# Attention with a gated convolution behind it: keys, queries and values loaded by groups of four heads

## The chip, the cores and the metric

The kernel runs on one core of a Trainium2 chip. The metric is the device time of one execution in microseconds (us); the time before is the median of three runs. The profile is that of one execution, and its span goes from the first to the last instruction.

## What is computed

`q`, `k` and `v` are float32 of 8 batches x 12 heads x 448 rows x 64. Attention has one more term in the denominator; its output, heads side by side, goes through a projection to three parts of 768, a convolution over the sequence by Fourier transform, two gates and a last projection:

```python
scores = scale * np.matmul(q, k.transpose(0, 1, 3, 2))
m = np.max(scores, axis=-1, keepdims=True)
e = np.exp(scores - m)
attn = e / (np.sum(e, axis=-1, keepdims=True) + np.exp(-m) + 1e-09)
x = np.matmul(attn, v)                        # then heads side by side: (8, 448, 768)
proj = x @ w_proj                             # three parts x1, x2, x3
x2_conv = np.fft.irfft(np.fft.rfft(x2, n=S, axis=1) * np.fft.rfft(filter_fft, n=S, axis=0), n=S, axis=1)
return (x1 * x2_conv * x3) @ w_out
```

## The kernel before, in words

The work is cut into tasks: a load, a set of matmuls, a copy out of PSUM. Each names its engine, what it needs and what it makes. A planner (`Plan`, the table `plan.ORDER`) fixes the order of the tasks on each engine when the program is built; `plan.FLIP` names the copies that go to the other of VectorE (DVE) and ScalarE (ACT). On the chip every engine then runs its own list in that order, and waits where an operand is not ready. Where the planner expects a hole in TensorE's early work, it puts filler matmuls on a tile of zeros (L1566, after 38 at the very start, L1574).

**Attention** goes by pairs of heads, 48 in all; i is the pair's number. Keys lie with the 64 features of two heads on the 128 partitions. For each pair there are three blocks of 128 keys (L947, four 64x64 matmuls to a set), and the last 64 keys of two neighbouring pairs share a fourth block (L952). Each set is followed by one exponential of 128x896 on ScalarE (L966), which writes an `e` buffer (seven of them) or, for the shared block, `er`. The outputs are 65 columns wide, since a column of ones beside the values gives the denominator: L977 for the shared rows, L997 for the three blocks. A tiny write (`sink` on ScalarE, `sinks` on GpSimd, L987) orders the two halves of a bank. VectorE divides (L1010 to L1012) into `xb`, and DMA transposes (L1056; TensorE in batch 0) make `xT`.

**The dense part** of a batch has the projections (L1175 for the convolved part, L1273 for the two gates), the transforms by tables `ft`, `fr`, `bt` (L1157, L1223, L1319), VectorE's products and sums between them, and the output projection L1091, whose result is copied to `osb` and stored by SP's queue (L1406, three buffers in turn).

**Loads of keys, queries and values** are what the change is about. Batches 0 and 1 are "staged" (`staged`): GpSimd's queue casts to bfloat16 on the way, four heads to a DMA (L544 queries in runs of 1024 B, L549 keys and values in runs of 768 B); the first two pairs come as float32 through SP's and ScalarE's queues and are cast by VectorE or GpSimd (L585, L591). TensorE turns keys and queries pair by pair (L621 to L642) and VectorE or ScalarE copies the turned blocks to `kT` and `qT` (L488, L486). Batches 2 to 7 are "loaded" (`loaded`): SP's queue brings each pair's keys and queries as float32 (L747, L727), GpSimd casts them (L759, L733), and DMA transposes on SP's queue turn them (L705 keys, L694 queries); GpSimd's queue brings the values (L754), and GpSimd copies them beside their ones (L771). The last 64 rows of keys and values come apart, in `rests`, in four DMAs of 256 B runs for the keys and four for the values of a batch (L509), and GpSimd casts them (L514, L719). The weights come by GpSimd's queue (L924, L929), the filter too (L836 to L840). The pads between the halves of the `e` buffers are zeroed by GpSimd (L1583, L1584).

## Time and profile before

| what | value |
| --- | --- |
| median of three runs | 372.58 us |
| lowest and highest run | 371.19 and 373.03 us |
| profiled execution, first to last instruction | 370.8 us |
| busy: TensorE, VectorE, ScalarE, GpSimd | 356.4, 274.8, 237.5, 127.6 us |
| DMA packets, bytes | 133958, 61.93 MB |

The execution that was profiled has no time of its own beside its span of 370.8 us; the runs' median lies 1.8 us above it. Rows of the profile name a line of the kernel, the engine, the operation, and the tiles written and read. "<-" at the end of a row names what ended the engine's idle time before it. PEld is TensorE's weight load, which overlaps its matmuls.

### The profile page before, as it was taken

The page shows a single profiled execution, that of the slowest core. Times are in us where ns is not written, and L with a number is a line of the kernel's source. Part 1 is how long each engine was busy: PE and PEld are TensorE (multiplying, and loading weights), DVE is VectorE, ACT ScalarE, POOL GpSimd, SP SyncE. Part 2 cuts the span into 40 slices and gives each one's busy share as a digit, 9 for nine tenths or more (in the row PEclk, how much of TensorE's full clock was granted, in tenths as well). Part 3 has the DMA queues.
Part 4 walks back from the last instruction along what each step waited for, and adds up shares of the span by engine and source line. Part 5 has one row for each costly group of instructions (what it writes and reads, how often), then busy time and mean ns, then how long its engine had stood idle before and what let it go on. Part 6 is the DMA issues. An engine that isn't in the chain of part 4 may idle for free. (4 is left out here: it accounts for less than half of the span.)

```text
span 370.8 us, 10707 instructions
## 1 busy us (share of the span) xinstructions
PE 356.4 (96%) x4300; PEld 211.8 (57%) x4300; DVE 274.8 (74%) x674; ACT 237.5 (64%) x379; POOL 127.6 (34%) x278
## 2 busy tenths in 40 slices
PE   7989999999999979999999999999999999999995
PEld 7666675554555545565555646665565655555552
DVE  5468659982789726897579977689459898779970
ACT  4999876756767548567565657867776561334343
POOL 9984251444625274265537523313100100000000
PEclk9999999999999999999999999999999999999999
DMA  9999999988999999999998799995830074125035
GB/s 169 194 191 204 207 207 205 206 169 160 168 242 156 229 214 208 235 242 192 206 182 202 166 245 192 262 208 122 171 72 1 7 196 89 42 45 170 4 129 172
DMA packets 133958, 61.93 MB, mean 167 GB/s; under 512 B 105165, under 2 KB 130704, under 8 KB 133904
## 3 DMA queue, kind: packets, MB, share of 16 engines
q1 hardware_dynamic: 111552, 48.71, 61.6%
q0 software_dynamic: 22112, 12.26, 25.4%
q8 instruction: 34, 0.56, 0.6%
q10 hardware_dynamic: 240, 0.23, 0.2%
q14 instruction: 20, 0.16, 0.2%
HBM read 43.86 MB, written 11.01 MB: 148 GB/s over the span
## 5 line engine op out<-in xcount | busy, mean ns | idle before, releaser
L966 ACT ACTIVATE e<-psum 128x896 bf16<-128x896 f32 x144 | 126.6, 920 | 40.8 <-PE psum L947 37.3
L1273 PE MATMUL psum<-xT,wproj_bf 128*128 128x448 bf16 x576 | 121.7, 353 | 0.1
L1273 PEld LDWEIGHTS <-wproj_bf 128*128 128x128 bf16 x576 | 53.4, 98 | 47.7 <-issue 5.0
L1091 PE MATMUL psum<-wout_bf,yT 128*128 128x384 bf16 x288 | 54.7, 326 | 0.8 <-DVE g L1288 0.4
L1175 PE MATMUL psum<-xf,wproj_bf 128*128 128x452 bf16 x252 | 53.9, 357 | 0.0
L947 PE MATMUL psum<-qT,kT 64*64 64x448 bf16 x576 | 45.4, 359 | 2.5 <-DVE g L1288 0.7
L997 PEld LDWEIGHTS <-e 128*128 128x128 bf16 x1152 | 42.0, 98 | 9.6 <-issue 5.2
L997 PE MATMUL psum<-vn,e 128*128 128x65 bf16 x1152 | 46.8, 194 | 0.0
L733 POOL CAST nat<-nat 112x512 bf16<-112x512 f32 x36 | 25.4, 708 | 44.7 <-DMA nat<-in_q_dram 41.8
L1241 DVE TENSOR_TENSOR t<-xs,hrs 113x768 bf16<-113x768 bf16 (+1 forms) x64 | 36.4, 578 | 2.9 <-ACT xs L486 2.3
L1288 DVE TENSOR_TENSOR g<-x,psum 128x448 bf16<-128x448 bf16 x48 | 29.2, 616 | 12.1 <-PE psum L1273 10.9
L1091 PEld LDWEIGHTS <-yT 128*128 128x128 bf16 x288 | 26.6, 98 | 19.9 <-issue 1.8
L1175 PEld LDWEIGHTS <-wproj_bf 128*128 128x128 bf16 x252 | 23.2, 96 | 22.2 <-issue 1.1
L486 ACT CAST x<-psum 128x448 bf16<-128x448 f32 (+1 forms) x39 | 20.4, 529 | 22.6 <-PE psum L1273 14.5
L759 POOL CAST nat<-nat 128x384 bf16<-128x384 f32 x36 | 21.5, 598 | 32.2 <-DMA nat<-in_k_dram 31.9
L486 ACT COPY osb<-psum 128x384 f32<-128x384 f32 x39 | 18.2, 486 | 20.1 <-PE psum L1091 15.9
L486 ACT CAST xs<-psum 113x384 bf16<-113x384 f32 (+1 forms) x41 | 19.2, 482 | 15.1 <-PE psum L1223 14.1
L1012 DVE TENSOR_TENSOR xb<-psum,den 128x896 bf16<-128x896 f32 x24 | 26.2, 1091 | 0.8
L486 ACT CAST cr<-psum 128x452 bf16<-128x452 f32 x35 | 18.0, 539 | 11.5 <-PE psum L1319 11.0
L947 PEld LDWEIGHTS <-kT 64*64 64x64 bf16 x576 | 15.6, 105 | 17.1 <-issue 12.9
L966 ACT ACTIVATE er<-psum 128x896 bf16<-128x896 f32 x24 | 22.2, 926 | 4.3 <-PE psum L952 3.5
L987 POOL MEMSET sinks<- 1x1 bf16 x18 | 1.6, 91 | 65.6 <-PE psum L977 65.6
(143 smaller groups left out, 501.3 us busy)
## 6 DMA issues: line engine op xcount, KB each, us to landing
nat<-in_q_dram SPq DMA_DIRECT2D x37, 224.0 KB, 3.8
out_dram<-osb SPq DMA_DIRECT2D x21, 384.0 KB, 3.5
nat<-in_k_dram SPq DMA_DIRECT2D x38, 192.0 KB, 3.9
nat<-in_v_dram POOLq DMA_DIRECT2D x15, 192.0 KB, 6.3
wproj_bf<-in_moe_w_proj_dram POOLq DMA_DIRECT2D x2, 1152.0 KB, 18.1
out_dram<-osb SPq DMA_DIRECT2D x12, 192.0 KB, 2.7
ks<-in_v_dram POOLq DMA_DIRECT2D x9, 192.0 KB, 4.9
rests<-in_k_dram SPq DMA_DIRECT2D x32, 48.0 KB, 4.3
```

The source lines that it names most:

```text
L486: nc.scalar.copy(to, of)
L733: lambda hp=hp, qsrc=qsrc: nc.gpsimd.tensor_copy(qn[:, hp].rearrange("p j (u d) -> p u j d", u=2), qsrc.rearrange("p (u j d) -> p u j d", ...
L759: lambda hp=hp, sv=sv: nc.gpsimd.tensor_copy(kn[:, hp // 2, 3 * (hp % 2) + 1 : 3 * (hp % 2) + 4].rearrange("p j (u d) -> p u j d", u=2), sv),
L947: nc.tensor.matmul(sc[r, u, 0:S], kT[b % 2][c, hp // 2, 3 * turned + t, r], qT[b % 2][c, hp, :])
L966: nc.scalar.activation(to, of, AF.Exp, scale=SCALE)
L997: nc.tensor.matmul(out_bank(u)[:, n + 3 * turned, :], P["e"][1 + t][:, o : o + 128], vn[b % 2][:, hp, 4 * u + t, :], start=False, stop=tur ...
L1012: nc.vector.tensor_tensor(W["xb", b][:, hp // 2].rearrange("p s (u d) -> p u s d", u=2), op[:, :, :, 0:DH], rec[:].unsqueeze(3).to_broadca ...
L1091: nc.tensor.matmul(ops[:n, :DCH], y[:, dt, 0:n], wout_bf[:, dt, ch * DCH : (ch + 1) * DCH], start=(dt == 0), stop=(dt == NDT - 1),)
L1175: nc.tensor.matmul(pps, wproj_bf[:, kt, D + dt * 128 : D + (dt + 1) * 128], W["xf", b][:, :, kt, 0:FQ], start=(kt == 0), stop=(kt == NDT - 1),
L1241: nc.vector.tensor_tensor(t[:K], L["xs", par, ch][:K], h, op=ALU.mult)
L1273: nc.tensor.matmul(p[:, :S], wproj_bf[:, kt, 2 * part * D + dt * 128 : 2 * part * D + (dt + 1) * 128], xT()[:, kt, 0:S], start=(kt == 0), ...
L1288: nc.vector.tensor_tensor(g[:, dt, :], L["x1", dt], p[:, :S], op=ALU.mult)
```

## The change

Four heads form a group: heads 2m, 2m+1, 2m+6 and 2m+7. A pair is now a head and the one six places on. A partition holds seven neighbouring rows of one head, so keys and queries of a group come in runs of 7 x 64 x 4 = 1792 B, two for each of 128 partitions, and the fourth of the seven rows is the shared key block. `rests` and its 64 DMAs are gone.

- Batches 0 and 1: one DMA on GpSimd's queue for a group's keys and one for its queries, 14 turns of 128x64 on TensorE for each, and one copy of 128x896 to `kqT`. Group 0 of batch 0 comes as four float32 loads of 64 partitions, three on SP's and one on ScalarE's queue, and is turned as float32 by 14 matmuls each with a float32 unit matrix (`eye`).
- Batches 2 to 7: one float32 load on SP for keys and one for queries of a group, one cast of 128x896 each on GpSimd, and one DMA transpose of 14 blocks for both, where before keys and queries had their own.
- Values of all batches come by GpSimd's queue in DMAs of 64 partitions with runs of 1024 B (four to a batch, eight in batch 0), cast on the way; one copy to a pair instead of two, and four small copies for the shared rows (eight in batch 0).
- The projection's weights come in two DMAs of 64 partitions each, since the heads stand in another order. The scores read their queries as seven runs of 64 columns. Every exponential puts the rows back in order as it writes. Before the branch SP has 113 instructions instead of 227 and GpSimd 219 instead of 277; TensorE has 23 fillers fewer, 140 bfloat16 turns instead of 160, and 56 float32 ones.
- `plan.ORDER` and `plan.FLIP` are new. The copies that make `fr` can now go to VectorE, and do; the `sink` writes of batch 0 go to GpSimd.

```diff
-    def rows(x, b, hp, n=2):
-        return bass.AP(x.tensor, x[b, 2 * hp].offset, [[3 * DH, 128], [S * DH, n], [1, 3 * DH]])
...
+    def group(x, b, m, par=None):
+        return bass.AP(x.tensor, x[b, 2 * m + (par or 0)].offset, [[PER * DH, 128 if par is None else 64], [NHP * S * DH, 2], [1, PER * DH]])
...
+    def v_load(b, h, n):
+        for r in range(2):
+            nc.gpsimd.dma_start(
+                vroom[64 * r : 64 * r + 64, DH * (4 * h + 1 - r) :][:, 0 : 4 * DH * n].rearrange("p (h x) -> p h x", h=n),
+                bass.AP(v.tensor, v[b, h].offset + 3 * DH * r, [[PER * DH, 64], [S * DH, n], [1, 4 * DH]]),
+            )
...
+    def kq_turn(src, hy):
+        tb = bank2(hy)
+        of = src.rearrange("p (u j d) -> p u j d", u=2, j=PER)
+        for j in range(PER):
+            for u in range(2):
+                nc.tensor.transpose(tb[64 * u : 64 * u + 64, j * 128 : (j + 1) * 128], of[:, u, j], ident_bf)
+
+    def kq_first(x, p, hy):
+        tb, c = bank(hy), slice(64 * p, 64 * p + 64)
+        of = first_kq[x][c].rearrange("p (u j d) -> p u j d", u=2, j=PER)
+        for j in range(PER):
+            for u in range(2):
+                nc.tensor.matmul(tb[64 * u : 64 * u + 64, j * 64 : (j + 1) * 64], of[:, u, j], eye[c, c])
...
+            for x, of in enumerate((k, q)):
+                at = 6 * (b - NSTAGED) + 2 * m + x
+                src = rooms[(2 + at) % 3]
...
+                add("SP", 0.5, 0.0, lambda of=of, src=src, m=m: nc.sync.dma_start(split(src), group(of, b, m)), need=free, make=[("s", b, m, x)],
+                    dma=1.18, run=60)
...
+            add("SP", 2.0, 0.0,
+                lambda m=m: nc.sync.dma_start(
+                    kqT[b % 2][:, m].rearrange("p x j n -> p (x j) n"), kqn[:, m].rearrange("p x j c -> p (x j c)"), transpose=True
+                ),
...
-        nc.gpsimd.dma_start(
-            wproj_bf[:, :, cs], moe_w_proj[:, cs].rearrange("(t p) c -> p t c", p=128)
-        )
+        for c in range(2):
+            nc.gpsimd.dma_start(
+                wproj_bf[64 * c : 64 * c + 64, :, cs], moe_w_proj[c * DCH : (c + 1) * DCH, cs].rearrange("(t p) c -> p t c", p=DH)
+            )
...
-                        nc.tensor.matmul(sc[r, u, 0:S], kT[b % 2][c, hp // 2, 3 * turned + t, r], qT[b % 2][c, hp, :])
+                        nc.tensor.matmul(sc[r, u, 0:S], kq[c, m, 0, 4 * d + t - 1, n], kq[c, m, 1, :, n])
```

**ScalarE, batch 0.** These are rows of ScalarE's list at its start; `e` and `er` are exponentials, `fr` a table, `sink` the tiny write, `kT` turned keys. Before:

```order
L486 COPY kT_89<-psum 128x384
L966 ACTIVATE e_97<-psum 128x2x448
L966 ACTIVATE e_96<-psum 128x2x448
L854 CAST fr<-psum 113x452
L855 ACTIVATE fr<-psum 113x226
L966 ACTIVATE e_98<-psum 128x2x448
L966 ACTIVATE e_99<-psum 128x2x448
L966 ACTIVATE e_100<-psum 128x2x448
L966 ACTIVATE er_103<-psum 128x896
L966 ACTIVATE e_101<-psum 128x2x448
L486 COPY kT_89<-psum 128x384
L966 ACTIVATE e_102<-psum 128x2x448
```

The same place after the change:

```order
L468 CAST kqT_89<-psum 128x7x64 x2
L789 ACTIVATE e_93<-psum 128x2x448
L789 ACTIVATE e_94<-psum 128x2x448
L789 ACTIVATE e_95<-psum 128x2x448
L789 ACTIVATE er_100<-psum 128x896
L789 ACTIVATE e_96<-psum 128x2x448
L789 ACTIVATE e_97<-psum 128x2x448
L789 ACTIVATE e_98<-psum 128x2x448
L789 ACTIVATE e_99<-psum 128x2x448
L789 ACTIVATE e_93<-psum 128x2x448
L468 COPY kqT_89<-psum 128x896
L789 ACTIVATE er_100<-psum 128x896
```

The fr copies and the second key copy have left the run of exponentials, and a copy of a whole group stands behind the ninth.

**GpSimd, the start.** Rows of GpSimd's list after the identity matrix; `vroom` holds values as they land, `vn` values beside their ones, `e` here is the zeroing of the pads. Before, the pads stand ahead of the first load:

```order
L1584 MEMSET e_102 128x64
L544 DMA nat<-in_q_dram 112x4x256
L549 DMA nat<-in_k_dram 128x4x192
L549 DMA nat<-in_v_dram 128x4x192
L591 CAST ldm<-nat 112x2x4x64
L585 CAST ldm<-nat 128x2x3x64
```

After the change ten loads and the first values stand ahead of them:

```order
L488 DMA vroom<-in_v_dram 64x3x256 x2
L537 DMA nat<-in_k_dram 128x2x448
L537 DMA nat<-in_q_dram 128x2x448
L1412 MEMSET vn_92 128x42
L537 DMA nat<-in_k_dram 128x2x448
L537 DMA nat<-in_q_dram 128x2x448
L537 DMA nat<-in_k_dram 128x2x448
L497 COPY vn_91<-vroom 128x2x3x64
L508 COPY vn_91<-vroom 64x2x64
```

The pads have moved from the front of the list to a place behind ten loads and the first copies of values.

**SP, around the first output stores.** Rows of SP's queue; `out_dram` is a store, `rests` the shared rows, `kT`, `qT` and `kqT` turns by DMA, `x` a turn of the dense part. Before, around the second store:

```order
L727 DMA nat<-in_q_dram 112x2x256
L747 DMA nat<-in_k_dram 128x2x192
L1406 DMA out_dram<-osb 128x768
L509 DMA rests<-in_v_dram 64x3x64 x4
L727 DMA nat<-in_q_dram 112x2x256 x2
L747 DMA nat<-in_k_dram 128x2x192
L705 DMA_TRANSPOSE kT_89<-nat 128x11x128
```

After the change, around the first three stores:

```order
L1011 DMA_TRANSPOSE x_2024<-ldm 128x12x128
L1229 DMA out_dram<-osb 128x768
L577 DMA nat<-in_k_dram 128x2x448
L1229 DMA out_dram<-osb 128x768
L587 DMA_TRANSPOSE kqT_90<-nat 128x14x128
L577 DMA nat<-in_k_dram 128x2x448
L1229 DMA out_dram<-osb 128x768
```

The four small loads are gone, and what stands before a store is one load of twice the size, or a turn of 14 blocks.

## The prediction

> **What bounds the kernel now.** The page comes first: who is busy, and is it even over the span?

> ```profile
> PE 356.4 (96%) x4300; PEld 211.8 (57%) x4300; DVE 274.8 (74%) x674; ACT 237.5 (64%) x379; POOL 127.6 (34%) x278
> PE   7989999999999979999999999999999999999995
> DMA  9999999988999999999998799995830074125035
> ```

> TensorE is busy for 96%, with thin slices only at the start and the end; the DMA engines are nearly full for two thirds of the span. The table by stretches sharpens this; its columns after the width are PE, weight loads, DVE, ACT and POOL.

> ```profile
> 0.00:10.00 10.00, 7.87 (x95) 6.78 (x95) 5.96 (x24) 5.29 (x8) 9.29 (x31) 1.00 1.00 170
> 10.00:30.00 20.00, 17.73 (x418) 12.62 (x419) 12.24 (x29) 18.96 (x29) 18.10 (x38) 1.00 1.38 193
> 30.00:100.00 70.00, 69.09 (x902) 41.89 (x899) 50.27 (x124) 51.48 (x85) 28.91 (x59) 1.00 1.11 194
> 100.00:200.00 100.00, 95.83 (x1166) 54.30 (x1164) 75.22 (x181) 66.16 (x100) 45.74 (x100) 1.00 1.13 210
> 200.00:300.00 100.00, 99.73 (x1252) 58.76 (x1254) 78.92 (x185) 68.04 (x106) 25.52 (x53) 1.00 0.71 143
> 300.00:361.00 61.00, 61.00 (x451) 34.59 (x451) 52.15 (x136) 24.04 (x47) 0.09 (x1) 1.00 0.34 95
> ```

> From 30 us on TensorE idles 0.91 us to 100, 4.17 us from there to 200, and 0.27 from there to 361. From 10 to 30 us ScalarE is the full engine (18.96 of 20) and TensorE's time is partly filler. So the change, which leaves the dense matmuls alone, can win in two places only: in ScalarE's run of exponentials before 30 us, and in TensorE's few waits after that. The waits view, TensorE from 30 to 361 us, names these:

> ```profile
> PE psum L977 <- DVE osb L488: 2.5, 2, 2.3
> PE psum L1223 <- DMA x<-ldm: 0.8, 1, 0.8
> PE psum L947 <- DVE g L1288: 0.7, 2, 0.5
> ```

> **The start.** ScalarE's timeline shows batch 0 (21 exponentials of 128x896):

> ```profile
> 8.74 1.73 ACT L966 ACTIVATE e<-psum 128x896 bf16<-128x896 f32 x2 [0.68 <-PE psum L947]
> 10.36 0.54 ACT L854 CAST fr<-psum 113x452 bf16<-113x452 f32 x1
> 10.93 0.36 ACT L855 ACTIVATE fr<-psum 113x226 bf16<-113x226 f32 x1
> 11.19 2.53 ACT L966 ACTIVATE e<-psum 128x896 bf16<-128x896 f32 x3
> 13.79 0.92 ACT L966 ACTIVATE er<-psum 128x896 bf16<-128x896 f32 x1
> 15.40 0.49 ACT L486 COPY kT<-psum 128x384 bf16<-128x384 bf16 x1
> 15.76 0.95 ACT L966 ACTIVATE e<-psum 128x896 bf16<-128x896 f32 x1
> 16.57 0.18 ACT L987 COPY sink<-one 1x1 bf16<-1x1 bf16 x1
> 21.68 0.18 ACT L987 COPY sink<-one 1x1 bf16<-1x1 bf16 x1
> 24.95 2.60 ACT L966 ACTIVATE e<-psum 128x896 bf16<-128x896 f32 x3
> 27.43 0.18 ACT L987 COPY sink<-one 1x1 bf16<-1x1 bf16 x1
> ```

> Three in 2.53 us, 0.92 each, start 0.81 us apart. The first starts at 8.74, the eighth at 15.76, and the last ends at 24.95 + 2.60 = 27.55. In this stretch the change takes from ScalarE the two fr copies (0.54 + 0.36), a key copy (0.49) and three sink copies (3 x 0.18): 1.93 us. It adds one copy of 128x896 from PSUM, which I price as an exponential of that size, 0.92. **Net -1.0 us.** The fr copies and four of the group copies go to VectorE, which has 7.8 us free between 10 and 30; if that cover were gone, the 0.9 would come back.

> Can the exponentials begin as early? The first group's keys and queries now come as four loads of 64 partitions, and TensorE turns them as float32, 14 matmuls a load, where before VectorE or GpSimd cast and TensorE turned in bfloat16. The last of the four old loads had landed when GpSimd cast it:

> ```profile
> 7.23 0.51 POOL L585 CAST ldm<-nat 128x384 bf16<-128x384 f32 x1
> 8.12 0.57 PE L947 MATMUL psum<-qT,kT 64*64 64x448 bf16 x8 [0.34 <-ACT kT L486]
> ```

> The four now move 917 KB instead of 850, so I keep 7.2 us. No row has a float32 matmul; the nearest are these:

> ```profile
> L642 PE MATMUL psum<-ident_bf,nat 112*64 112x112 bf16 x80 | 3.7, 212 | 0.0
> L997 PE MATMUL psum<-vn,e 128*128 128x65 bf16 x1152 | 46.8, 194 | 0.0
> ```

> Packed, they take 3.7/80 = 46 ns each, so 14 take 0.65 us at least; one by one at 212 ns they take 3.0. I take twice the lower end, 1.3, since the operand has twice the bytes and these too go to two halves of the array. The scores of the first head pair stand behind all four turns: 7.2 + 1.3 = 8.5, and 0.62 later (8.12 to 8.74) the first exponential, 9.1 instead of 8.74. The eighth could then start at 9.1 + 7 x 0.81 = 14.8.

> [...]

> The eighth waits for something else as well. GpSimd zeroed the pads of the e buffers from 1.71 to 4.07 us (the first and the last of 14 rows below); now it issues ten loads first, and the eighth score stands in TensorE's queue behind the outputs of the first pair, which need the pads.

> ```profile
> L549 POOL DMA_DIRECT2D nat<-in_v_dram x6 | 4.8, 809 | 0.0
> L544 POOL DMA_DIRECT2D nat<-in_q_dram x5 | 3.7, 743 | 0.0
> L598 POOL COPY vn<-nat 128x192 bf16<-128x192 bf16 x24 | 8.1, 375 | 9.1 <-DMA nat<-in_v_dram 9.0
> ```

> ```profile
> 1.71 0.27 POOL L1583 MEMSET e<- 128x128 bf16 x1
> 3.92 0.15 POOL L1584 MEMSET e<- 128x64 bf16 x1
> ```

> Its queue begins near 1.9 us: ten issues of 0.78 each (7.8), a memset of 0.3 on either side of the copies (0.6), one value copy of 384 elements (twice 0.34, 0.7), four small ones (1.0 together), and the pads of the three buffers that the first outputs read (six memsets, which overlap; 14 took 2.36, so 1.0): 13.0. The outputs take 16 small matmuls (0.3) and 24 x 41 ns (1.0), a score and the step to ScalarE 0.6, so the eighth exponential starts near 14.9, where ScalarE itself is ready for it at 14.8, against 15.76. From there 13 remain on either side: 11.8 us before (to 27.55), of which 12 x 0.81 + 0.92 = 10.6 are exponentials, 0.54 sinks and 0.6 waits. After the change 10.6 + 0.92 and none to all of those waits: 26.4 to 27.0, middle 26.7. **The start is worth -0.8 us**, between -1.5 (the first exponential no later than now, no waits) and +1.5 (float32 at 212 ns each, pads after the tenth issue's landing).

> **TensorE's own work.** 160 bfloat16 turns become 140, and 56 float32 ones: 20 x 46 ns less, 56 x 46 to 212 ns more: +1.7 to +11 us. They lie before 30 us, where ScalarE sets the pace, with one exception, the 14 counted above; and 23 fillers fewer stand there. Without that cover it would be +3.6 at 80 ns each. I count 0. The moving operand of the scores is now seven runs of 64 columns; no row shows such a read, so 0, with 0 to 672/4 x 20 ns = 3.4 us (a tenth of their 0.2 us a set) kept for the range.

> **TensorE's waits.** The longest, 2.3 us at 132, is this chain:

> ```profile
> 124.15 0.47 SPq L747 DMA_DIRECT2D nat<-in_k_dram  x1
> 124.72 0.41 SPq L1406 DMA_DIRECT2D out_dram<-osb  x1
> 125.17 2.75 SPq L509 DMA_DIRECT2D rests<-in_v_dram  x4
> 131.66 1.02 DVE L488 COPY osb<-psum 128x384 f32<-128x384 f32 x2 [3.81 <-DMA out_dram<-osb]
> ```

> A store, issued at 124.72 behind two loads, frees its buffer only near 131.6; the median store needs 3.5 us:

> ```profile
> out_dram<-osb SPq DMA_DIRECT2D x21, 384.0 KB, 3.5
> nat<-in_q_dram SPq DMA_DIRECT2D x37, 224.0 KB, 3.8
> rests<-in_k_dram SPq DMA_DIRECT2D x32, 48.0 KB, 4.3
> ```

> VectorE stands on that buffer for 3.81 us, and TensorE behind VectorE. The 64 small loads of shared rows go, SP issues 113 rows of program instead of 227 before the branch, and keys and queries come in runs of 1792 B instead of 768, 1024 and 256 B. That speaks for fewer late stores; loads of 448 KB instead of 192 or 224 standing before a store speak for longer waits at one place. Of the 2.5 + 0.8 us that late transfers cost now, I take half as gone, **-1.6 us**, between -3.3 and +5.

> **GpSimd in the steady part** casts 36 pieces of 896 elements instead of 72 smaller ones, within its 66% idle; a late one would stop a turn, whose group is needed a batch later. 0.

> **Sum.** 370.8 (span) - 0.8 - 1.6 = 368.4. The median of the runs shown, 372.58, lies 1.8 us above that span, for what lies around it and between runs; I carry this over: **370.2 us**.

> **The rivals.** *The gain is eaten* (0.26): float32 turns or pads cost what ScalarE saves, or stores are late as often as now: 371.0 with the first alone, 371.8 with the second alone, 372.6 with both. For it speaks that the eighth exponential gains only 0.9 us and hangs on GpSimd's queue; against it, that three small items leave ScalarE whatever else happens. *The coarse queue* (0.31): SP issues in order, and now a store or the transposes of x stand behind 14-block turns and 448 KB loads, twice what stood there; from the point at which one lands 2 us later than its reader can bear, TensorE idles as at 132. At 0.8 to 2.3 us a hit, and one in each of the last six batches, and with the 1.6 not gained: 370.2 + 1.6 + 6 x 0.8 = 376.6 at the low price; three hits as long as the one at 132 would cost as much. Against it: fewer transfers in all, and a DMA share of 0.71 and less from 200 us on. *A clean start and no late store* (0.07): -1.5 and -3.3: 367.8. That the change does not do what it says is excluded for its operations, which the built order shows.

> **How the numbers follow.** The forecast, a little faster, has 0.36, and with the clean start 0.43. A measurement of this kernel tells about 0.5% (1.9 us) from no change; the forecast is 2.4 us below the median, so both count as faster, 0.43. The eaten gain counts as same, 0.26, the coarse queue as slower, 0.31. The likeliest case alone spans 368.5 to 371.5. The range takes in the clean start less 1.3 us for short stalls that no row names, 366.5, and the coarse queue with one or two hits more, 378.

> **What would show it.** Right: the first exponential near 9.1, the eighth near 14.9, batch 0's last ending near 26.7, and no wait on osb over 1 us. Wrong: float32 turns of over 100 ns each, a first exponential after 10, TensorE idling over 6 us between 100 and 300, or waits on x and xT transfers that are not there now.

## The result, and the profile after

The changed kernel takes 388.51 us, the median of four runs (386.44 to 392.78), the kernel before 371.88 (four runs, one more than above, 370.89 to 373.03). The ratio is **1.042, with a 95% interval of 1.0373 to 1.0468**: slower, by 16.6 us, where 370.2 was predicted, and outside the range of 366.5 to 378. The longest of the four runs, 392.78 us, is left out of the ratio as a slow one, and it is the one that was profiled, so sums of its rows below have to be set against 391.0 - 370.8 = 20.2 us, the difference of the two spans.

The page of the kernel after: who is busy, and the slices of TensorE, of its granted clock and of the DMA engines.

```profile
PE 367.5 (94%) x4369; PEld 216.8 (55%) x4369; DVE 275.0 (70%) x665; ACT 237.3 (61%) x375; POOL 115.1 (29%) x220
PE   7998999969995999989999999999899999999993
PEclk9699999969999899999999999999999999999998
DMA  9699999996999949989597999993620056035034
```

The clock row held nothing but nines before. Now slices 2, 9 and 14 are at six, six and eight tenths; the last two lie in or next to a hole of TensorE's row. The DMA engines have new thin slices; the first of them is the second, where they were full before. The table by stretches shows both.

```profile
10.00:15.00 5.00, 5.00 (x82) 4.11 (x81) 2.62 (x7) 1.88 (x3) 1.97 (x8) 0.50 1.22 196
15.00:20.00 5.00, 5.00 (x95) 2.89 (x93) 1.69 (x3) 4.37 (x6) 3.46 (x17) 0.83 0.08 10
30.00:100.00 70.00, 65.52 (x907) 40.41 (x907) 49.84 (x120) 47.18 (x69) 32.64 (x57) 0.95 1.09 198
100.00:200.00 100.00, 93.42 (x1042) 51.83 (x1041) 73.19 (x165) 62.61 (x101) 32.28 (x52) 0.98 1.01 211
200.00:300.00 100.00, 97.61 (x1238) 56.11 (x1237) 74.73 (x176) 67.13 (x103) 28.53 (x52) 1.00 0.77 151
```

From 10 to 15 us TensorE is busy all the time, at half its clock, and ScalarE works for 1.88 of 5 us. From 15 to 20 the DMA engines move 10 KB a microsecond instead of some 200. TensorE idles 4.5 us from 30 to 100, 6.6 from there to 200 and 2.4 to 300, against 0.9, 4.2 and 0.3 in the same stretches before.

**What TensorE waits for**, from 30 to 361 us:

```profile
PE psum L1046 <- DMA x<-ldm: 5.8, 3, 4.2
PE psum L914 <- DMA wout_bf<-in_moe_w_out_dram: 3.3, 1, 3.3
PE psum L1046 <- DMA x<-nat: 2.1, 3, 1.0
```

L1046 is L1223 of the kernel before, the transform that reads the second transpose of x (DMA transpose L1011). The wait on `osb`, 2.5 us before, is gone, as forecast. In its place stand 7.9 us on transposes of x and 3.3 on the output weights. The sum of the prediction had nothing for either.

**What a wait costs beyond itself.** These are the three stretches in which the granted clock was one half:

```profile
9.85:16.68 6.83, 6.83 (x99) 4.86 (x98) 3.21 (x7) 3.10 (x6) 2.27 (x10) 0.50 0.94 152
81.53:88.36 6.83, 5.67 (x18) 2.60 (x18) 0.91 (x4) 0.48 (x1) 2.27 (x5) 0.50 1.26 246
125.91:129.32 3.41, 3.41 (x28) 2.00 (x25) 1.77 (x4) 1.73 (x3) 0.00 (x0) 0.50 1.30 272
```

TensorE was busy for 6.83, 5.67 and 3.41 us of them. If that work takes half as long at the full clock, 3.4 + 2.8 + 1.7 = **7.9 us** are lost. This is an estimate, two fifths of the 20.2 us, and rather an upper one: 25 turns that took 2.93 us here took 1.67 in e1 at the full clock. In the execution of the kernel before that was profiled, the clock fell to one half only in the last stores, at 370.16 us.

**The start**, TensorE's timeline. L567 is the float32 turn; the profile shows each as two records, so 28 are one load's 14.

```profile
5.67 1.37 PE L567 MATMUL psum<-ldm,nat 64*64 64x64 f32 x28
8.32 1.03 PE L567 MATMUL psum<-ldm,nat 64*64 64x64 f32 x28 [0.95 <-DMA nat<-in_k_dram]
9.82 2.93 PE L567 MATMUL psum<-ldm,nat 64*64 64x64 f32 x50
12.45 0.58 PE L770 MATMUL psum<-kqT 64*64 64x448 bf16 x2
12.54 0.53 PE L567 MATMUL psum<-ldm,nat 64*64 64x64 f32 x6
```

The second set of turns waits until 8.27 us for its load, a key load that SP issues last of its three. The other two sets, whose loads landed at 5.39 and 6.45, stand behind it in TensorE's list and run at half the clock, 2.93 us for 25 turns. The first exponential starts at 13.49 us instead of 8.74:

```profile
13.49 1.73 ACT L789 ACTIVATE e<-psum 128x896 bf16<-128x896 f32 x2 [3.12 <-PE psum L770]
20.85 1.73 ACT L789 ACTIVATE e<-psum 128x896 bf16<-128x896 f32 x2 [0.87 <-PE psum L770]
```

The eighth starts at 20.85, and batch 0's last ends at 33.5 (27.55 before). **GpSimd's timeline** says why the DMA engines ran dry at the same time (L1406 are the pads of the `e` buffers, L488 the next batch's value loads, L745 the projection's weights):

```profile
14.46 0.20 POOL L1406 MEMSET e<- 128x128 bf16 x1 [2.19 <-ACT e L789]
15.27 0.20 POOL L1406 MEMSET e<- 128x128 bf16 x1 [0.51 <-ACT e L789]
16.79 0.20 POOL L1406 MEMSET e<- 128x128 bf16 x1 [1.23 <-ACT e L789]
18.51 1.25 POOL L488 DMA_DIRECT2D vroom<-in_v_dram  x2
27.72 1.32 POOL L745 DMA_DIRECT2D wproj_bf<-in_moe_w_proj_dram  x2
```

The pads now stand behind the first exponentials and wait for three of them, 3.9 us, and the loads behind the pads wait with them. The lateness goes on: the first load of batch 2 on SP's queue is issued at 55.72 us (41.6 before), and the output weights at 69.53, which land at 82.64, where TensorE has waited 3.3 us for them.

**A transpose of x.** SP's queue and TensorE around the longest wait:

```profile
116.48 2.97 SPq L1011 DMA_TRANSPOSE x<-ldm  x1
```

```profile
120.75 0.55 PE L820 MATMUL psum<-vn,e 128*128 128x65 bf16 x12
125.46 0.32 PE L1046 MATMUL psum<-x,ft 113*113 113x384 bf16 x1 [4.16 <-DMA x<-ldm]
125.62 1.29 PE L820 MATMUL psum<-vn,e 128*128 128x65 bf16 x24
```

The transpose is issued 0.7 us after the last copy of its source, and TensorE has run out of other work in its list 4 us before it lands. That is the rule, not one mishap. I took all 14 second transposes of x, from the end of the last copy of their source (medians):

| kernel | landed after | first reader starts after | readers that start within 0.15 us of the landing |
| --- | --- | --- | --- |
| before | 4.7 us | 9.2 us | 1 of 14 |
| after | 4.5 us | 5.4 us | 7 of 14 |

The transposes are not slower. Their readers stand closer behind them.

### The profile page after: what moved, and what is told of

Read it like the earlier page. It is cut to its first block, busy times and chain, and to the rows that moved or that the text cites. A ratio compares the mean times of both kernels' runs of the same rounds, so it can differ in the third digit from the quotient of the medians.

```text
span 391.0 us, 10602 instructions
## 1 busy us (share of the span) xinstructions
PE 367.5 (94%) x4369; PEld 216.8 (55%) x4369; DVE 275.0 (70%) x665; ACT 237.3 (61%) x375; POOL 115.1 (29%) x220
## 5 line engine op out<-in xcount | busy, mean ns | idle before, releaser
L914 PE MATMUL psum<-wout_bf,yT 128*128 128x384 bf16 x288 | 56.5, 338 | 3.5 <-DMA wout_bf<-in_moe_w_out_dram 3.3
L581 POOL CAST nat<-nat 128x896 bf16<-128x896 f32 x36 | 34.4, 966 | 71.0 <-DMA nat<-in_k_dram 26.9
L770 PE MATMUL psum<-kqT 64*64 64x448 bf16 x576 | 47.1, 365 | 1.1 <-DVE g L1111 0.8
L914 PEld LDWEIGHTS <-yT 128*128 128x128 bf16 x288 | 27.8, 100 | 24.8 <-issue 9.3
L468 ACT CAST xs<-psum 113x384 bf16<-113x384 f32 (+1 forms) x45 | 20.9, 482 | 25.7 <-PE psum L1046 23.6
L468 ACT COPY osb<-psum 128x384 f32<-128x384 f32 x36 | 17.0, 483 | 21.8 <-PE psum L914 19.2
L497 POOL COPY vn<-vroom 128x384 bf16<-128x384 bf16 x48 | 26.2, 575 | 13.1 <-DMA vroom<-in_v_dram 9.9
L770 PEld LDWEIGHTS <-kqT 64*64 64x64 bf16 x576 | 15.3, 106 | 19.3 <-issue 16.3
L1046 PE MATMUL psum<-x,ft 113*112 113x384 bf16 (+1 forms) x56 | 17.0, 342 | 8.6 <-DMA x<-ldm 5.8
L488 POOL DMA_DIRECT2D vroom<-in_v_dram x36 | 23.4, 661 | 3.2 <-DMA wproj_bf<-in_moe_w_proj_dram 2.1
## 6 DMA issues: line engine op xcount, KB each, us to landing
out_dram<-osb SPq DMA_DIRECT2D x21, 384.0 KB, 3.5
```

The lines of the kernel that those rows point to most:

```text
L468: nc.scalar.copy(to, of)
L497: nc.gpsimd.tensor_copy(to[:, :, 0:3, 0:DH], of)
L581: lambda x=x, m=m, src=src: nc.gpsimd.tensor_copy(kqn[:, m, x].rearrange("p j (c d) -> p c j d", c=2), src.rearrange("p (c j d) -> p c j d ...
L770: nc.tensor.matmul(sc[r, u, 0:S], kq[c, m, 0, 4 * d + t - 1, n], kq[c, m, 1, :, n])
L914: nc.tensor.matmul(ops[:n, :DCH], y[:, dt, 0:n], wout_bf[:, dt, ch * DCH : (ch + 1) * DCH], start=(dt == 0), stop=(dt == NDT - 1),)
```

## The experiments

Tasks have numbers, and `plan.ORDER` gives each a rank. Most experiments move a few tasks by giving them another rank, in this form, with the rest of the kernel as after:

```diff
     add = plan.add
+    plan.ORDER = tuple({14: 9, 17: 13}.get(n, x) for n, x in enumerate(plan.ORDER))
```

Below only the numbers are given. Each run was profiled once, and the rows are those of that one execution. All ratios are to the kernel before on the same chip, whose median was 371.73 to 373.82 us.

### The start: e1 to e4

**e1** exchanges SP's two key loads of the first group (tasks 14 and 17, above), so that the one whose turns stand second comes second.

> Only the order of two of SP's first loads is exchanged, so that the key load that TensorE turns second lands second and not last. If the late start comes from that place in TensorE's list: no idle of 0.95 us before the second set of float32 turns, TensorE's clock stays at 1.0 to 15 us, the first exponential starts near 11.3 us instead of 13.5, and the run takes 386 to 388 us (up to 2.3 less than the 388.3 of the change, less where TensorE then only waits longer for the output weights at 79 us). If the float32 turns themselves set it: the first exponential stays above 12.5 and the time within 1 us.

380.9 us, ratio 1.0205 (1.0121 to 1.0288). The first exponential starts at 10.42, the clock is full from 5 to 20 us, and at equal work TensorE is within 1 us of the kernel before up to 56 us. **By the medians the exchange is worth 7.6 us, but much of that hangs on the half clock.** e2 and e3 below leave these loads as they were in after. In their profiled executions TensorE waited 0.5 and 0.4 us ahead of the second turns instead of 0.95, the clock stayed full there, the first exponential started at 11.56 and 11.49, and the spans are 385.0 and 383.3 us, against 383.2 of e1. In after and e4 the clock fell at the start, and the spans are 391.0 and 390.0. How much the exchange gives alone is not shown. TensorE's later waits hardly changed:

```profile
PE psum L1046 <- DMA x<-ldm: 5.6, 3, 3.7
PE psum L914 <- DMA wout_bf<-in_moe_w_out_dram: 2.1, 1, 2.1
PE psum L1046 <- DMA x<-nat: 1.8, 3, 1.1
```

So the rest, about 9 us, is something else, and it begins after 60 us.

**e2** puts the pads ahead of the exponentials (`{11: 39}`), **e3** also lets ScalarE write three sinks of batch 0 (`plan.FLIP` with 260, 285, 310 added), **e4** leaves these and loads the output weights earlier (`{226: 297}`).

> The pads' zeroing moves ahead of GpSimd's tenth load, as it stood ahead of the exponentials before the change. If the pads' wait for three exponentials held up the loads behind it: no wait of GpSimd for ScalarE's e, the value loads now issued at 18.5 us are issued near 13, and the DMA engines are no longer empty between 16 and 19 us; the time falls by 1 to 3 us (385 to 387). If the sink write that stands between those loads holds them anyway: only the first pair of loads moves, the next stay near 19 to 20 us, and the time stays within 1 us of 388.3.

> The pads as in the run before, and the three sink writes of batch 0 go back to ScalarE, 0.18 us each there. If GpSimd's in-order list is what makes batch 1's loads, the projection weights and at last the output weights late: loads issued from 13 us on without a gap, the first projection weights issued near 22 us instead of 27.7, the output weights near 63 us instead of 69.5, TensorE's wait for them under 1 us and no half clock after it; 380 to 384 us. If the lateness is that of the large loads themselves: the output weights still land after 78 us and the time falls by less than 2 us.

> Only the load of the output weights moves, ahead of the value loads of batch 2 on GpSimd's queue. If its place behind a value copy that waits for its own load is what costs: issued near 59.5 us, landed near 70, TensorE's wait of 3.3 us at 79 us and the half clock of the 6 us behind it are gone, 5 us less: 382 to 384 us. If the engines are simply full there: the value and key loads land later in its place, TensorE waits elsewhere, and the time falls by less than 2 us.

None helped by the medians: 391.29 (386.21 to 396.38), 390.65 (385.12 to 398.28, ratio 1.0484) and 392.13 us (1.0511, 1.0418 to 1.0605). Each did its own part. In e2 GpSimd's wait for exponentials is gone and in e3 the projection's weights are issued at 20.1 us instead of 27.7. But in e3 GpSimd then stands 11.7 us at a later sink, and the output weights land at 78.8 all the same. In e4 they land at 70.3 and nobody waits for them; a key transpose in the same stretch does:

```profile
PE psum L770 <- DMA kqT<-nat: 6.4, 1, 6.4
PE psum L1046 <- DMA x<-ldm: 4.8, 3, 2.5
```

### One wait at a time, from e1: e5 to e12

All of these have e1's exchange. **e5** adds fillers (30 ahead of the first output projection, 55 ahead of a transform of batch 1), to keep the clock up through two waits. This is one of the two places; `warm_up` issues that many matmuls on zeros:

```diff
-                L["O", st, ch] = bank(hy)
+                L["O", st, ch] = bank(hy); warm_up(bank(hy), 30 if (b, st, ch, calm) == (0, 1, 0, True) else 0)
```

**e6** adds e3's edits. **e7** moves batch 4's value loads behind a transpose of x that was late beside them (`140: 630, 141: 631`). **e8** is e6 with SP's first loads of batch 2 and the output weights earlier (`77: 50, 79: 270, 82: 276, 226: 297`).

> The exchanged key loads, and filler matmuls on zeros in TensorE's list ahead of the two long waits that are left: 30 ahead of the first output projection (wait of 2.1 us for its weights at 74 us) and 55 ahead of the transform that waits 3.7 us for its transposed operand at 114 us. The fillers do no work of the kernel. If the half clock behind such a wait is a cost of its own: the two stretches of 3.4 us at half clock (76.5 and 117.5 us) are gone, and with them 1.6 us each: 377 to 378 us against 380.2 with the exchange alone. If only the waits count: within 1 us of 380.2.

> The exchanged key loads, the pads ahead of GpSimd's tenth load and batch 0's sink writes on ScalarE. If GpSimd's list at the start is a cause by itself: value loads issued from 12.5 us on, the first projection weights near 20 us (23.4 with the exchange alone), the output weights 2 us earlier and TensorE's wait for them gone, 377 to 378.5 us. If TensorE is not waiting for these loads in the first place: the loads come earlier, the output weights stay where a later value copy holds them (near 64 us), and the time is within 1 us of 380.2.

> The exchanged key loads, and the value loads of batch 4 (four of 192 KB, which GpSimd issued from 110.7 us on) put some 10 us later in GpSimd's list. If they delay the transposes that land at 117.7 us: these land near 114, TensorE's wait of 3.7 us and the half clock behind it are gone, 375 to 377 us. If it is SP's own queue of 448 KB loads and 14-block transposes ahead of them (the coarse queue of the prediction): they land after 116.5 us as before, and the time stays within 1 us of 380.2.

> All on the loads together: the exchange, pads and sink writes as before, SP's first load of batch 2 where its room is free (near 15 us) and its second ahead of the third, and the output weights ahead of batch 2's values. If batch 1 and 2's loads are late because in-order lists hold them while the DMA engines idle: engines full from 10 us on, output weights landed before 70 us, no wait of TensorE for them nor for kqT, 374 to 377 us. If the engines are the limit: the wait moves to kqT as when the output weights alone were moved (6.4 us), and the time is 380 us or more.

| kernel | median, us | ratio (95%) | what became of the wait |
| --- | --- | --- | --- |
| e5 | 383.19 | 1.0182 (1.0094 to 1.0269) | half clock at 117 us gone; 1.9 us for a key transpose at 70, half clock 69 to 76 |
| e6 | 382.9 | 1.0224 (1.0146 to 1.0303) | pads and first sinks gone; 11.7 us of GpSimd at a later sink, output weights still 2.3 us late |
| e7 | 386.37 | 1.0297 (1.0217 to 1.0377) | the transpose landed 4.9 us after the end of its issue instead of 5.8, TensorE's wait for it 1.8 us instead of 3.7, half clock still; a key transpose 5.6 us late at 74 |
| e8 | 390.94 | 1.0447 (1.0379 to 1.0515) | output weights in time; a key transpose 3.6 us late, x 3.4 |

In e7 the value loads beside that transpose explain a part of its lateness at most. The time did not fall.

**e9** has two more sinks on ScalarE (358, 381); **e10** adds e8's earlier loads of batch 2 to that; **e11** is e1 with a transpose of xT and a key load behind the transpose of x that was late (`464: 577, 132: 578`); **e12** is e10 and e11 together.

> As the run with exchanged keys, early pads and batch 0's sink writes on ScalarE, and the sink writes of pairs 8 and 10 on ScalarE too (0.18 us each there). If GpSimd's waits of 7 to 12 us for TensorE ahead of these two writes are what keeps the output weights and batch 2's values late: no such wait, batch 2's value loads issued near 45 us instead of 56, the output weights landed before TensorE asks for them at 75 us; 377 to 379 us where before takes 372. If batch 2's lateness comes from SP's queue (its first load waits for batch 1's last group): the values come earlier, the first transposes of batch 2 still land after 65 us, and the time stays at 381 to 382.

> As the run before, and SP's first two loads of batch 2 ahead of the one that waits for batch 1's last group. If the two in-order lists together hold the loads while the DMA engines idle: no second from 10 to 60 us in which they move under 100 KB, the first transposes of batch 2 landed before 62 us, no wait of TensorE over 1 us between 60 and 80 us, no half clock there; 375 to 378 us. If the transfers themselves are the limit: a wait of 2 us or more for kqT or for the output weights stays between 66 and 80 us, and the time is over 379.

> The exchanged key loads, and on SP the second transposes of batch 1's convolved part ahead of the x transposes of batch 2 and of the query load of 448 KB that stood ahead of them. If SP's queue of large transfers delays them (the coarse queue of the prediction): they land 3 us or more earlier against their last source copy (9.2 us behind it with the exchange alone), TensorE's wait of 3.7 us near 114 us is under 1.5, no half clock there; 377 to 379 us. If they take that long whatever stands ahead: within 1 us of the lag and within 1 us of the exchange alone.

> All edits together: keys, pads, the five sink writes, SP's first loads of batch 2 and its order at the transposes. If each wait was a place in an in-order list: both long waits and their half clock gone, 371 to 375 us, about as before the change. If the waits only move to the next late transfer: 378 us or more.

They took 383.45 us (1.0251), 383.16 (1.0238, 1.0179 to 1.0298), 388.8 (1.0401) and 387.37 (1.0366). In e10 no wait over 1.5 us is left from 60 to 80 us and no half clock there, and it gained nothing on e1. In e11 the transpose that was moved ahead landed 5.5 us after its source instead of 9.2 and its wait went; two other transposes of x were late instead, 2.75 us at 105 and 3.3 at 139, with half clocks at both. In e12 the longest wait, 3.4 us, is for VectorE's gates. **The waits that were taken away came back elsewhere, mostly at another transfer.** Part of that is chance: up to 74 us the lists of e5 and e7 are those of e1, and yet the first key transpose of batch 2 landed 4.1 us after its issue in e1, 6.5 in e5 and 8.3 in e7, and TensorE waited 0, 1.9 and 5.6 us for it. Waits that come back fit a list with no room anywhere. They would also fit a layout whose larger transfers are slow wherever they stand. The next two runs tell these apart.

### Layout or list: e13 and e14

**e13** keeps the change's layout and gives the tasks, from about 40 us on, the order of the kernel before, as far as the same tasks exist; `plan.ORDER` and `plan.FLIP` are new tables, and the planner reckons with transfers that land 0.4 to 3 us later when it places fillers. **e14** is the other way round: the kernel before, whole, with 11 of its 14 second transposes of x later in SP's list and nothing else moved on any engine:

```diff
     add = plan.add
+    plan.ORDER = tuple({1108: 521.5, 1119: 563.5, 1243: 799.5, ..., 1910: 1887.5}.get(n, x) for n, x in enumerate(plan.ORDER))
```

> The change's data layout whole (groups of four heads, 448 KB loads, 14-block transposes, values by GpSimd's queue), its keys loaded as in e1, but from about 40 us on the tasks of every engine stand in the order of the kernel before as far as the same tasks exist, and the transposes of x and of keys stand well ahead of their first readers again (6 to 14 us instead of 4 to 6). Theory 'the new list leaves transfers no room': waits on transposes of x under 1.5 us in all, no half clock between 20 us and the last stores, 372 to 376 us. Rival 'the layout itself, large transfers in few queues, is slower whatever the order': the waits on x, kqT or wout come back at other places, over 5 us in all, and the time is 380 us or more.

> The kernel before, with nothing of the new layout; only 11 of its 14 second transposes of x stand later in SP's list, so that about 5 us instead of 8.7 lie between the last copy of their source and their first reader, as in the change. Theory 'room': TensorE waits 0.5 to 2 us at several of them, the granted clock falls to half behind the longer ones, +3 to +9 us. Rival 'layout': in the old layout SP's queue and the DMA engines carry a tighter list without harm, within 1.5 us of the kernel before.

**e14: 383.75 us, ratio 1.0276 (1.0199 to 1.0354)**, 12 us by the medians, more than I had expected. The old layout, with its small loads, loses as much as the new one does after its start, once its transposes have no room:

```profile
PE psum L1223 <- DMA x<-ldm: 5.5, 4, 2.2
PE psum L1175 <- ACT ldm L486: 3.1, 1, 3.1
PE psum L977 <- ACT ldm L486: 1.8, 1, 1.8
```

```profile
105.92:109.33 3.41, 3.41 (x16) 1.47 (x13) 2.76 (x7) 1.24 (x3) 0.00 (x0) 0.50 1.02 246
146.88:150.29 3.41, 3.41 (x28) 2.04 (x29) 1.18 (x2) 1.97 (x4) 1.83 (x5) 0.50 1.12 316
232.21:235.62 3.41, 3.41 (x40) 2.35 (x42) 0.62 (x1) 1.85 (x4) 2.40 (x5) 0.50 0.33 83
```

Four waits on the transposes themselves, two on ScalarE, which could not write the next source while the last one still waited for its transpose, and behind three of them 3.41 us at half the clock: 10.4 us of waits and, by the estimate used above, 5.1 of lost clock, against some 3.3 and none before. Only the order of SP's list differs.

**e13: 383.55 us, ratio 1.0322 (1.0238 to 1.0406).** It did not come to the 372 to 376 us that the theory gave. Its readers stand 9.2 us behind their sources and none of 14 starts at the landing, and TensorE waits for no transpose or load for over 0.5 us. But it was 5 us behind already at 60 us (its exponentials before 33 us start up to 5 us later than in e1), and two waits of 2.4 and 2.3 us on copies by ScalarE, each with 3.41 us at half clock, make the rest. Those copies had in turn waited for a transpose of x to let go of its source:

```profile
184.34 0.54 ACT L468 CAST ldm<-psum 128x452 bf16<-128x452 f32 x1 [4.57 <-DMA x<-ldm]
184.94 1.14 PE L914 MATMUL psum<-wout_bf,yT 128*128 128x384 bf16 x6 [2.26 <-ACT ldm L468]
```

So room at the reader alone does not do; the next writer of the source needs it too.

### Both cures together: e15 to e18

**e15** and **e16** have e1's first 30 us and room behind it, in two orders found apart from each other, with new `plan.ORDER` and `plan.FLIP` and e13's allowance for late landings. **e17** is e16 with four value loads moved two casts later in GpSimd's list. **e18** is e16 with two readers of one late transpose moved behind 12 matmuls of the gates.

> The change's layout with e1's order for the first 30 us (key loads exchanged, pads of the e buffers behind one load less) and an order with room behind it, as in e13 (all transposes of x, keys and queries and all loads placed several us ahead of their readers). Theory 'room': e1 was 0 to 0.5 us behind the kernel before at 56 us, and e13 lost only about 2.5 us after that point, so 371 to 376 us, no half clock between 15 us and the last stores or one of 3.4 us at most. Rival 'layout': single waits of 2 us and more with half clocks come back at new places, 379 us or more, as in every list of the new layout so far.

> A second order found apart from that of e15 by the same two rules (e1's first 30 us; room behind every transfer from there on), to see whether the rules or one lucky order make the time. Theory 'room': 371 to 376 us as well, within 1% of e15. Rival 'layout': 379 us or more, or far from e15 in either direction.

> e16 was 0.9 us behind the kernel before at 151 us, then a transpose of x landed 9.4 us after its issue and TensorE waited 2.8 us for it, with 3.4 us at half clock behind. Four value loads of 192 KB were issued in the same moment as that transpose; here they stand two casts later in GpSimd's list, nothing else moves. Theory 'the value loads crowd the transpose': it lands 4 to 5 us after its issue, no wait and no half clock at 155 to 161, 373 to 375 us. Rival 'what else stands in SP's queue there': it lands as late, 377 to 379 us.

> e16 with the two readers of that transpose moved behind 12 matmuls of the gates that need nothing from it (2.3 us of TensorE's work at full clock), the transfers as they were. Theory 'room': the wait falls from 2.8 to under 1 us, the half clock behind it goes (1.7 us), together 3 to 4 us: 374 to 376 us, whatever makes the transpose late. If the time stays at 378, the single wait was not what e16 still lost.

| kernel | median, us | ratio (95%) | waits of 1.2 us and more between 30 and 361 us | half clock |
| --- | --- | --- | --- | --- |
| e15 | 378.26 | 1.0139 (1.0084 to 1.0194) | 1.9 on `er`, 1.2 on a sink | 3.4 us |
| e16 | 378.29 | 1.0115 (1.0053 to 1.0178) | 2.8 on x | 3.4 us |
| e17 | 379.76 | 1.0197 (1.0148 to 1.0247) | 1.8 on a key transpose | none |
| e18 | 377.24 | 1.0102 (1.0049 to 1.0155) | 1.4 on VectorE's gates | none |

Two orders within 0.1 us of each other, 10 us faster than the change with the same layout: **the lists (their order, with what it brings in fillers and in the choice between VectorE and ScalarE) make at least 10 of the 16.6 us.** In e16 TensorE was 0.9 us behind the kernel before at 151 us. Then came this, on SP's queue and on TensorE:

```profile
145.55 2.38 SPq L1011 DMA_TRANSPOSE x<-ldm  x1
```

```profile
157.33 0.33 PE L1046 MATMUL psum<-x,ft 113*113 113x384 bf16 x1 [2.81 <-DMA x<-ldm]
157.49 4.11 PE L1096 MATMUL psum<-xT,wproj_bf 128*128 128x448 bf16 x12
```

The transpose landed 9.4 us after the end of its issue, and 12 matmuls of the gates, which took 2.43 us at the full clock in after (from 114.76 us), took 4.11. Four value loads of 192 KB had been issued in the same moment. In e17, where they come later, the same transpose landed 3.5 us after the end of its issue, with no wait. So here, in one execution each, the transpose beside the value loads landed 5.9 us later; in e7 it was 0.9 us, at another place. But e17 lost more elsewhere: a wait of 1.8 us for keys at 73 us, which stands ahead of the edit and so is chance, and 4 us between 180 and 215. In e18 the loads stay, the readers have room, and wait and half clock are gone, but its 1 us is within the intervals. Its clock is full to the end and no wait is over 1.4 us:

```profile
PE 362.2 (96%) x4387; PEld 215.1 (57%) x4387; DVE 276.9 (74%) x667; ACT 234.7 (62%) x374; POOL 117.9 (31%) x219
PEclk9999999999999999999999999999999999999999
```

**What stays open** is this last 1%. TensorE idles 376.4 - 362.2 = 14.2 us in e18's profile and 370.8 - 356.4 = 14.4 in that of before, so over the whole span what is left stands in its busy time, 5.8 us more. The rows of instructions do not show one cause for it. The scores, which read seven runs of 64 columns, are busy for 47.3 us instead of 45.4 (45.7 to 47.4 in the other kernels of the new layout). Transposes hold SP's queue longer: 12 of e18's 46, 7 of them of 14 blocks, take over 3 us to issue, up to 7.25, against 4 of 60 before. By time there is one place: at equal work e17 and e18 are 2 us behind the kernel before at 180 us and 6 behind from 215 to the end. The kernel before does not idle in that stretch, e18 does for 3 us. e18's row, then that of before:

```profile
180.00:215.00 35.00, 32.03 (x362) 18.22 (x360) 26.38 (x61) 20.39 (x34) 14.43 (x23) 1.00 1.22 186
180.00:215.00 35.00, 35.00 (x417) 20.15 (x416) 28.47 (x63) 23.22 (x38) 20.24 (x40) 1.00 1.01 189
```

No run separates these from faults of my orders, and no order of the new layout beat the kernel before.

## Why the prediction was wrong, point by point

**Two steps failed. The first is the one that priced the start**: "The scores of the first head pair stand behind all four turns: 7.2 + 1.3 = 8.5". The first exponential came at 13.49 instead of 9.1, 4.4 us late, and three things add up to that. The last of the four loads landed at 8.27 and not at 7.2, 1.1 us later (between 7.8 and 9.5 in the other kernels of the new layout). I had compared bytes alone; GpSimd's queue, which no longer has the pads ahead of it, now issues its first load at 1.62 us instead of 4.01, and that this is the reason is not shown. Next, the sum took the four loads and their turns for a queue in the order of landing, but the new list has the turns of the last-landing load second, as its order shows. From that landing to the first exponential e1 takes 1.9 us, as the sum had it (1.3 + 0.62), and e2, in the old order and at the full clock, 3.7: 1.8 us more. The last 1.5 us are the clock, which the sum left out: in after it halved at 9.85 us, after a wait of 0.95 us in thin work, and the same way took 5.2.

The size of a float32 turn was right: 1.03 to 1.37 us for 14 against the 1.3 taken, 70 to 100 ns each. Twice the lower end was my estimate; the runs show the time and not what makes it.

**The pads** were expected to be ready for the first outputs, so that the eighth exponential starts at 14.9. I had them behind ten issues and one pair's copies; in the list they stand behind three exponentials, and GpSimd waited for these. e2 and e3, in which this wait is gone, are no faster by the medians; what it did was to empty the DMA engines from 15 to 20 us, which moved 10 KB a microsecond in after, 85 in e2 and 163 in e3.

**TensorE's own work, 0**: right in kind. The turns lie beside other work once the start is in order, since e1 is level with the kernel before at 56 us. The scores, with the moving operand in runs of 64, are busy for 0.3 to 2.0 us longer, inside the 0 to 3.4 kept for it. That the runs make this is not shown: at the full clock one such matmul takes 360 to 361 ns (e17, e18), against 359 before.

**The second failed step is TensorE's waits, -1.6**: the late store is gone, as forecast, and no wait on `osb` over 1 us came back. But the term asked only what the removed loads had made late. The new list puts the readers of x 5.4 instead of 9.2 us behind their sources, and that came to 7.9 us of waits on x in place of 0.8. Waits on transfers of 7.9 + 3.3 = 11.2 us stand in place of 2.5 + 0.8 = 3.3, so not -1.6, between -3.3 and +5, but +7.9, before the clock's part.

**GpSimd in the steady part, 0**: wrong. "Within its 66% idle" is an average. Its list is served in order, so a sink or a pad that waits holds the loads behind it: 11.7 us at one sink in e3 and e6, the output weights 15 us later than before.

**The rivals.** *The coarse queue* had the right sign and named "waits on x and xT transfers that are not there now" as its sign, which came. Its mechanism fits only in part: transposes of x landed as fast as before (4.5 us against 4.7), and e14 shows the same loss with the old, fine queue. Key transposes of 14 blocks do land later, a median of 5.9 us after their issue instead of 4.3. Its price, 0.8 us a hit, left out the half clock that came with some hits: by the estimate above up to 1.7 us beside each of e13's waits of 2.4 and 2.3 us, and 2.8 beside that of 3.3 in after. *The eaten gain* and *the clean start* did not come. What none of the cases held was that a new order is a change of its own, larger than the change of layout that it came with.

**The range** went to 378 and the time was 388.5. It added the start's bound and the queue's bound as rivals; here both came, and with each the clock fell to one half, at 9.85 us and at 125.91.

## What to carry to other kernels

When a change brings a new order with it, price the order apart: for each transfer that the critical engine reads, count what stands in that engine's list between the source and the reader, before and after, and take the profile's landing times against it. On an engine near 100% busy look at the granted clock behind a wait as well: in e13 the waits of 2.4 and 2.3 us came each with 3.41 us at half clock, by estimate up to 1.7 us more. A wait that was removed alone here mostly only showed the next late transfer. And one profile is one execution: the same list put the same transfer 4 us apart in three of them.

## What the runs showed of the hardware

**Float32 turns.** The 56 turns stand in the trace of after as 112 records of 64x64, and 14 of them took 1.03 us at full clock (from 8.32 us).

**Loads of 64 partitions.** In the first 10 us, in which the first four loads landed and the first values were issued, all of 64 partitions, the kernel after moved 170 KB a microsecond, as the kernel before did with its loads of 112 and 128 partitions and its shared rows. GpSimd's queue also issued six loads of 128 partitions in that stretch, from 2.98 to 8.75 us, so what the smaller ones reached alone is not shown.
